# Linear attention times SwiGLU in fp32 on one core: the first part's products and side-work matmuls tied to the written order, the reciprocals in two halves, the masked sum split one place ahead

## The chip, the cores and the metric

The kernel runs on one core of one Trainium2 chip. The metric is device time in microseconds, the median of several runs. Engines are named as in the profile: PE is TensorE (matmuls), PEld its weight loads, DVE is VectorE, ACT is ScalarE, POOL is GpSimd, SP is SyncE, which here issues DMAs only.

## The reference, cut to what matters

```python
xn = _layernorm(x)                                   # x: 2048 x 1024
q, k, v = (xn @ wqkv), in 32 heads of 32
phi = lambda t: jnp.where(t > 0, t + 1, jnp.exp(t)) + 1e-6
pq, pk = phi(q), phi(k)
kv = jnp.einsum("bhsd,bhse->bhde", pk, v);  z = jnp.einsum("bhsd->bhd", pk)
o = jnp.einsum("bhqd,bhde->bhqe", pq, kv) / (jnp.einsum("bhqd,bhd->bhq", pq, z)[..., None] + 1e-6)
s = o @ wo
h = _silu(xn @ w1) * (xn @ w3)                       # w1, w3: 1024 x 3584
return x + s * _silu(h @ w2)
```

All of it is fp32. Most of the arithmetic is in the products of `xn` with `wqkv`, `w1` and `w3` (the first part) and in `h @ w2` and `o @ wo` (the second).

## The kernel before

**Products.** Each fp32 operand is split into a high and a low half (`split`, L83: a copy on ACT makes the high half, a subtraction on DVE the low one), and `mm3` (L94) makes three fp32r matmuls of 128x128 by 128x512 of a pair. `product` (L378) does that for four pieces of the inner dimension: twelve matmuls into one PSUM bank. `gemm` (L399) makes a 2x2 block product from seven such products in Strassen's manner (Winograd's form). It is written in the order B11, T2, T3, T1, B21, T4, B22; the names are those of the weights' combinations, which `Operands.made` (L308) makes a stage ahead. The first product's bank is copied to `u` by ACT, later ones are added to `u` by DVE; B21 goes into the same bank as B11, after the copy; T4 into T3's and B22 into T1's. For two early pairs of keys and values (`early`) B21 comes second.

**The first part** (`half`, L525, twice: 1024 tokens each) runs these products for keys, values, queries and then gate and up (14 pairs of 256 columns). An accumulator's name tells which: `ak0_2` is bank a of the keys of half 0, pair 2; `bk`, `ck`, `dk` are its banks b, c and d (T2 goes into b, T3 and T4 into c, T1 and B22 into d); `v`, `q`, `g`, `u` stand for values, queries, gate and up.

**Side work** goes between the products: `catch_up` (L387) is called once behind nearly every product, and takes one step of a list. One list (`later`) holds, for each pair of keys and values, five steps (`keys_values`): turning a tile of keys and one of values by transposes (`trk`, `trv`, L481), which ACT copies from PSUM into the tile `kvr` (L482, two copies), and one step later the small product `kv` of the two (L514). The `kvr` tile comes from the same pool of eight buffers (`pb`) as the split weights; which buffer a tile gets, the framework decides while it schedules. The other list (`jobs`) is made of generators, which give up their turn at each `yield True`: in half 0 the next half's rows are normalised on DVE (`xn`, L154) and turned (`tA`, L218), then the sums of `w2` are made; in half 1 come the denominators (`den`, L754; their operands `pqs` are split at L91 and L92; the reciprocal at L762 and the store of `r_d`), the merging of `kv` into `wo` (`wp`; the masked sum `kvf`, its split `kvm`, the split of `wo` called `wos`), the division of the queries for the first half of the tokens, and the denominators of the second half.

**What sets the order.** The framework schedules by a simulated timeline: within each engine it puts first what it holds to be ready, unless an edge forbids it. `tc.issue_after(m)` adds such edges: what is traced under it, on m's engine, stands behind m in that engine's order. It is an order, and no wait of its own. Before the change, `catch_up` gave its steps edges to the sums of the products just made (`marks`, on ACT and DVE) and to weight loads (`fetched`, on SP); nothing tied one product to another on PE in the first part. Every engine runs its instructions in the order that was fixed at build time.

**The second part** (L865 on) multiplies `h` by `w2` in four segments and the divided queries by the merged `wo` in a fifth, eight groups of tokens each, with an edge from each product to the one before.

Of the kernel before, what the change touches and what calls it, by code (L numbers as in the profile page):

```python
# [17 lines left out]
C = 512  # L18
H = 32
# [3 lines left out]
def tile_linear_attention_times_swiglu(  # L23
# [10 lines left out]
    nc = tc.nc  # L34
# [250 lines left out]
    fetched, made = [], {}  # L285
# [89 lines left out]
                    else:  # L375
                        yield

    def product(acc, B, A, start, stop=True):  # L378
        K = ND // 2
        for k in range(K):  # L380
            mm3(acc, (B[:, 0, k], B[:, 1, k]), (A[:, 0, k], A[:, 1, k]),
                start=start and k == 0, stop=stop and k == K - 1)

    later = []
    jobs = []

    def catch_up(*marks):  # L387

        if later:
            later.pop(0)()  # L390
        elif jobs:
            job, in_order = jobs[0]
            with ExitStack() as behind:
                for m in marks + (tuple(fetched) if in_order else ()):
                    behind.enter_context(tc.issue_after(m.ins))
                if next(job, None) is None:
                    jobs.pop(0)

    def gemm(B, A, use, early=False, paired=False, own=False):  # L399

        name = B.name
        B.upto("B11")
        u = (st.tile([P, C], F32, tag="own", bufs=1, name=f"u{name}") if own else
             pe.tile([P, C], F32, tag="u", name=f"u{name}"))  # L410
        ba = bank(f"a{name}")
        product(ba, B.upto("B11"), A["A11"], True)
        copied = nc.scalar.copy(out=u, in_=ba)
        if early:
            catch_up(copied)
            yield
            product(ba, B.upto("B21"), A["A12"], False)
            use(0, 0, ba)
            yield
            for _ in B.stages:  # L420
                pass
        else:
            next(stages, None)
            catch_up(copied)
            if paired:
                yield
        bb, bc, bd = (bank(f"{n}{name}") for n in "bcd")
        product(bb, B.upto("T2"), A["S2"], True)
        added = nc.vector.tensor_add(out=u, in0=bb, in1=u)
        next(stages, None)  # L430
        catch_up(copied, added)
        if paired:
            yield
        product(bc, B.upto("T3"), A["S3"], True)
        c22 = small(f"c22{name}")
        added = nc.vector.tensor_add(out=c22, in0=bc, in1=u)
        next(stages, None)
        catch_up(copied, added)
        if paired:
            yield  # L440
        product(bd, B.upto("T1"), A["S1"], True)
        added = nc.vector.tensor_add(out=c22, in0=bd, in1=c22)
        use(1, 1, c22)
        next(stages, None)
        catch_up(copied, added)
        if paired:
            yield
        if not early:
            product(ba, B.upto("B21"), A["A12"], False)
            use(0, 0, ba)  # L450
            next(stages, None)
            catch_up(copied, added)
        if paired:
            yield
        product(bc, B.upto("T4"), A["A22"], False)
        c21 = small(f"c21{name}")
        made[name, "c21"] = added = nc.vector.tensor_add(out=c21, in0=bc, in1=u)
        use(0, 1, c21)
        next(stages, None)
        catch_up(copied, added)  # L460
        if paired:
            yield
        product(bd, B.upto("B22"), A["S4"], False)
        c12 = small(f"c12{name}")
        made[name, "c12"] = added = nc.vector.tensor_add(out=c12, in0=bd, in1=u)
        use(1, 0, c12)
        next(stages, None)
        if name[0] in "gu":
            catch_up(copied, added)
# [264 lines left out]
    def denominators(c):  # L734

        den = []

        def load(j):
            t = job_tile([P, 2, C], f"pqd{j}_{c}")
            nc.sync.dma_start(out=t, in_=pq_d[j // JG][c][:, j % JG:j % JG + 2])  # L740
            return t

        def steps(j, t):
            a = []
            for e in range(2):
                a.append(pb.tile([P, 2, C], FR, tag="b", name=f"pqs{j + e}_{c}"))
                split(a[e], t[:, e], 1e-6)
                yield True
            if not den:
                den.append(bank(f"den{c}"))  # L750
            for e in range(2):
                o = (j + e) * 2 * H
                for i in range(2):
                    nc.tensor.matmul(den[0], lhsT=zb[0][:, o:o + P], rhs=a[e][:, i], skip_group_check=True,  # L754
                                     start=j + e + i == 0, stop=j + e == ND - 1 and i == 1)
            yield True
            if j + 2 == ND:

                r = small(f"r{c}")
                nc.scalar.copy(out=r[:H], in_=den[0][H:2 * H])  # L760
                nc.vector.scalar_tensor_tensor(r[:H], den[0][:H], 1e-6, r[:H], op0=ALU.add, op1=ALU.add)
                nc.vector.reciprocal(r[:H], r[:H])  # L762
                nc.gpsimd.dma_start(out=r_d[c], in_=r[:H])

        return [Job(lambda j=j: load(j), lambda t, j=j: steps(j, t)) for j in range(0, ND, 2)]
# [26 lines left out]
    def merge_wo(k):  # L792

        both = []

        def load(e):
            j = k + e * (ND // 2)
            t = job_tile([P, 2, C], f"wo{j}")
            nc.sync.dma_start(out=t, in_=wo[j * P:(j + 1) * P, :].rearrange("p (n c) -> p n c", c=C))
            return t  # L800

        def steps(e, t):
            both.append(t)
            j = k + e * (ND // 2)
            f = small(f"kvf{j}")[:, :P]
            nc.vector.tensor_mul(f, hmask, kvacc[:, j])
            kvm = st.tile([P, 2, P], FR, tag="kvm", bufs=1, name=f"kvm{j}")
            split(kvm, f)
            o = [pb.tile([P, 2, C], FR, tag="b", name=f"wos{j}_{n}") for n in range(2)]
            for n in range(2):  # L810
                split(o[n], t[:, n])
                yield True
            yield True
            for n in range(2):
                acc = bank(f"wp{j}_{n}")
                mm3(acc, (kvm[:, 0], kvm[:, 1]), (o[n][:, 0], o[n][:, 1]), True, True)
                nc.scalar.copy(out=t[:, n], in_=acc)
                yield True
            if e:
                b = [t[:, n] for t in both for n in range(2)]  # L820
                for n, i in (("B11", 0), ("B21", 2), ("B22", 3)):
                    store(n, b[i])
                yield True
                yield from sums_of(*b)
                yield True
                for n, i in (("T1", 0), ("T3", 1), ("T4", 2), ("T2", 3)):
                    store(n, b[i])
                for _ in range(2):
                    yield True

        def store(n, t):
            nc.gpsimd.dma_start(out=wp_d[n][:, k], in_=t)

        return [Job(lambda e=e: load(e), lambda t, e=e: steps(e, t)) for e in range(2)]


# [81 lines left out]
    def second_weight(i, n, k):  # L918
# [4 lines left out]
                      lambda m, n, i=i: ho_d[i][m // NT][:, m % NT, KEPT.index(n)])  # L923
# [4 lines left out]
    acc = [home.tile([P, 2 if m < NG - 1 else 1, 2, C], F32, tag=f"acc{m}", name=f"acc{m}")  # L928
           for m, home in enumerate(homes)]
# [97 lines left out]
    X, xs = {}, []  # L1027
# [32 lines left out]
    for j, (i, m, n) in enumerate(sequence):  # L1060
        seg = segments[i]
        if n == ORDER[0]:
            parts[m] = attention_tokens(seg, m) if seg is attention else layer_tokens(seg, m, i == 0)
        fetch(j + AHEAD)
        with ExitStack() as order:
            for o in made[i, m, n]:
                order.enter_context(tc.issue_after(o.ins))
            b, start = next(parts[m])
        with ExitStack() as order:
            if j:  # L1070
                order.enter_context(tc.issue_after(multiplied.ins))
            multiplied = seg.product(b, X.pop(j), n, start)
        if m == NG - 1 and i + 1 < len(segments):
            segments[i + 1].place(n)
            segments[i + 1].right(n)
        elif m < NG - 2 and 0 < i < len(layers):
            catch_up(*loads, *made[sequence[j + AHEAD]])
        if j % 2 and (j + 5) // 2 < len(ORDER):
            first_right((j + 5) // 2)
        if n == ORDER[-1]:  # L1080
            next(parts[m])
# [24 lines left out]
```

## Time and profile before

| | us |
|---|---|
| median of 3 runs | 2388.78 (2388.39 to 2388.79) |
| the profiled execution, its own time | 2381.99 |
| its span, first to last instruction | 2380.1 |
| PE busy in the span | 2332.4 |
| DVE busy | 1633.6 |
| ACT busy | 938.0 |

The profiled execution is 6.8 us shorter than the median of the timed runs. The first part ends at about 1670 us of the span. A matmul's record is longer than its turn, since matmuls are pipelined: how fast they follow each other is read from their starts. In rows of the timeline the first number is the start, the second the length, and a bracket at the end gives the idle time of the engine before the row and what ended it. In the views of the profile buffer numbers are left out, so `ak0_2` reads `ak` with the number of its instruction.

### The profile page before, as it was taken

The numbers are of one execution on the slowest core, as the hardware profiler recorded it, in microseconds if no ns is written. First come the engines' busy times: TensorE is split into PE (matmuls) and PEld (weight loads), VectorE is DVE, ScalarE is ACT, GpSimd is POOL, SyncE is SP. The second block draws the span as 40 slices with busy tenths as digits, with TensorE's granted clock in tenths as the row PEclk, the third lists the DMA queues.
The fourth block names the chain that finished last, engine by engine and source line by source line (L and its number), as shares of the span: only waits on it lengthen the run. The fifth ranks groups of instructions, "written<-read, shape, count | busy, mean of one in ns | idle before, by whom it ended". The sixth has DMA issues, their size and how long they took to land.

```text
span 2380.1 us, 29741 instructions
## 1 busy us (share of the span) xinstructions
PE 2332.4 (98%) x10544; PEld 1928.1 (81%) x10544; DVE 1633.6 (69%) x2906; ACT 938.0 (39%) x1595; POOL 289.4 (12%) x359
## 2 busy tenths in 40 slices
PE   7999999999999999999999999999999999999998
PEld 5888888888888888888788888888888887788787
DVE  8755678878888575567877878778436566575644
ACT  5433544443332244445344333344435233243532
POOL 3000111212112110000222212211000000000001
PEclk9999999999999999999999999999999999999999
DMA  3222444547676572433444545544437565554656
GB/s 124 89 97 101 152 151 165 193 155 256 229 240 240 178 271 89 146 118 123 155 165 142 204 157 195 179 143 168 152 98 245 161 192 175 184 189 144 179 155 146
DMA packets 267365, 395.45 MB, mean 166 GB/s; under 512 B 17488, under 2 KB 191824, under 8 KB 266768
## 3 DMA queue, kind: packets, MB, share of 16 engines
q1 hardware_dynamic: 239248, 301.51, 38.9%
q0 software_dynamic: 27968, 92.03, 11.1%
q8 instruction: 83, 1.36, 0.2%
q14 instruction: 66, 0.54, 0.1%
HBM read 271.58 MB, written 140.77 MB: 173 GB/s over the span
## 4 chain that ended last, share of the span: by engine, by line
PE 86%; issue 7%; DMA 3%; DVE 1%; POOL 1%; ACT 1%; SPq 0%; POOLq 0%; DVEq 0%; ACTq 0%
PE cB L99 2%; PE cB L97 2%; PE cB L98 2%; PE dB L99 1%; PE dB L97 1%; PE dB L98 1%; PE kv L514 1%; PE aB L97 1%; PE aB L99 1%; PE aB L98 1%; PE cs L97 1%; PE cs L99 1%; PE cs L98 1%; DMA XA12s<-qs_d 1%; PE den L754 1%
## 5 line engine op out<-in xcount | busy, mean ns | idle before, releaser
L636 POOL DMA_DIRECT2D ho_d<-hs x112 | 101.7, 908 | 84.3 <-DVE hs L609 61.3
L628 POOL DMA_DIRECT2D ho_d<-sg x56 | 51.1, 912 | 446.4 <-DVE sg L623 373.0
L787 POOL DMA_DIRECT2D qs_d<-qd x32 | 27.3, 858 | 534.2 <-DVE qd L611 488.9
L587 POOL DMA_DIRECT2D pq_d<-pq x32 | 17.6, 550 | 483.2 <-DVE pq L475 478.7
L914 DVE TENSOR_TENSOR XA12B<-XA12B 128x512 fp32r<-128x512 f32 (+1 forms) x32 | 19.7, 623 | 53.2 <-ACT XA12B L913 53.2
L626 POOL DMA_DIRECT2D ho_d<-sg x56 | 37.9, 677 | 130.8 <-DVE sg L623 116.3
L97 PE MATMUL aB<-B21B,XA12B 128*128 128x512 f32 x112 | 44.6, 398 | 3.0 <-ACT XA12B L913 2.9
L97 PE MATMUL cB<-T4B,XA22B 128*128 128x512 f32 x112 | 43.8, 391 | 2.4 <-ACT XA22B L913 2.4
L97 PE MATMUL cB<-T2B,XS2B 128*128 128x512 f32 x112 | 44.0, 393 | 1.6 <-ACT cB L967 1.5
L97 PE MATMUL dB<-T1B,XS1B 128*128 128x512 f32 x112 | 44.3, 396 | 1.2 <-ACT XS1B L913 1.2
L99 PE MATMUL dB<-T1B,XS1B 128*128 128x512 f32 x112 | 44.1, 394 | 0.6 <-DVE XS1B L914 0.6
L99 PE MATMUL aB<-B21B,XA12B 128*128 128x512 f32 x112 | 44.4, 397 | 0.0
L98 PE MATMUL aB<-B21B,XA12B 128*128 128x512 f32 x112 | 44.3, 396 | 0.0
L99 PE MATMUL cB<-T4B,XA22B 128*128 128x512 f32 x112 | 43.9, 392 | 0.1
L98 PE MATMUL dB<-T1B,XS1B 128*128 128x512 f32 x112 | 44.0, 393 | 0.0
L99 PE MATMUL cB<-T2B,XS2B 128*128 128x512 f32 x112 | 43.8, 391 | 0.1
L99 PE MATMUL dB<-B22B,XS4B 128*128 128x512 f32 x112 | 43.7, 390 | 0.0
L99 PE MATMUL cB<-T3B,XS3B 128*128 128x512 f32 x112 | 43.7, 390 | 0.0
L98 PE MATMUL cB<-T2B,XS2B 128*128 128x512 f32 x112 | 43.6, 390 | 0.0
L98 PE MATMUL cB<-T4B,XA22B 128*128 128x512 f32 x112 | 43.6, 389 | 0.0
L97 PE MATMUL cB<-T3B,XS3B 128*128 128x512 f32 x112 | 43.6, 389 | 0.0
L98 PE MATMUL dB<-B22B,XS4B 128*128 128x512 f32 x112 | 43.6, 389 | 0.0
(5750 smaller groups left out, 7990.6 us busy)
## 6 DMA issues: line engine op xcount, KB each, us to landing
ho_d<-hs POOLq DMA_DIRECT2D x112, 256.0 KB, 5.8
qs_d<-qd POOLq DMA_DIRECT2D x32, 512.0 KB, 4.1
ho_d<-sg POOLq DMA_DIRECT2D x56, 256.0 KB, 3.5
w<-in_B_w SPq DMA_DIRECT2D x56, 256.0 KB
wt_d<-w SPq DMA_DIRECT2D x28, 512.0 KB
pq_d<-pq POOLq DMA_DIRECT2D x32, 256.0 KB, 2.8
a_dS<-xo SPq DMA_DIRECT2D x16, 512.0 KB
pqd<-pq_d SPq DMA_DIRECT2D x16, 512.0 KB
```

The costliest lines, as they stand in the source:

```text
L97: nc.tensor.matmul(acc, lhsT=wh, rhs=ah, start=start, stop=False, skip_group_check=True)
L98: nc.tensor.matmul(acc, lhsT=wh, rhs=al, start=False, stop=False, skip_group_check=True)
L99: return nc.tensor.matmul(acc, lhsT=wl, rhs=ah, start=False, stop=stop, skip_group_check=True)
L514: nc.tensor.matmul(acc, lhsT=r[:, 1, t], rhs=r[:, 0, t], start=t == 0, stop=t == C // P - 1)
L587: nc.gpsimd.dma_start(out=pq_d[j // JG][2 * h + c][:, j % JG], in_=pq)
L626: nc.gpsimd.dma_start(out=ho_d[i][2 * h + c][:, :, 0, k], in_=halves[:, :, 0])
L628: nc.gpsimd.dma_start(out=ho_d[i][2 * h + c][:, :, 1:3, k], in_=halves)
L636: nc.gpsimd.dma_start(out=ho_d[i][2 * h + c][:, :, 3 + 2 * e:5 + 2 * e, k], in_=o[e].rearrange("p (g n s) -> p g n s", n=2, s=P))
L754: nc.tensor.matmul(den[0], lhsT=zb[0][:, o:o + P], rhs=a[e][:, i], skip_group_check=True, start=j + e + i == 0, stop=j + e == ND - 1 and i ...
L787: nc.gpsimd.dma_start(out=qs_d[m][:, :, k], in_=t.rearrange("p a (n s) -> p (a n) s", s=P))
L914: return high, nc.vector.tensor_sub(out=lo, in0=src, in1=hi.bitcast(F32))
```

## The change

- `product` ties its matmuls behind the last matmul of the product made before (`multiplied`), except in the early gemms (`free`); a product that is made so becomes the next one's mark.
- `catch_up` ties what its step issues on PE behind the last product made, too: transposes, `kv`, `den` and `wp` can't stand ahead of it. They can still stand later than written.
- The reciprocal of 32x512 is made in two halves of 32x256, and each has a turn of its own ahead of it: two more `yield True` at the end of each of the four chunks of denominators.
- In `merge_wo` a turn is given up between the split of the masked sum and that of `wo`: eight more turns.
- In the second part the mark becomes a list; its edges are the same.

```diff
+    multiplied = []
+
+    def product(acc, B, A, start, stop=True, free=False):
         K = ND // 2
-        for k in range(K):
-            mm3(acc, (B[:, 0, k], B[:, 1, k]), (A[:, 0, k], A[:, 1, k]),
-                start=start and k == 0, stop=stop and k == K - 1)
+        with ExitStack() as order:
+            for m in () if free else multiplied:
+                order.enter_context(tc.issue_after(m.ins))
+            for k in range(K):
+                last = mm3(acc, (B[:, 0, k], B[:, 1, k]), (A[:, 0, k], A[:, 1, k]),
+                           start=start and k == 0, stop=stop and k == K - 1)
+        multiplied[:] = [last]
...
         if later:
-            later.pop(0)()
+            with ExitStack() as behind:
+                for m in multiplied:
+                    behind.enter_context(tc.issue_after(m.ins))
+                later.pop(0)()
         elif jobs:
...
-                for m in marks + (tuple(fetched) if in_order else ()):
+                for m in marks + tuple(multiplied) + (tuple(fetched) if in_order else ()):
...
-        product(ba, B.upto("B11"), A["A11"], True)
+        product(ba, B.upto("B11"), A["A11"], True, free=early)
...
-                nc.vector.reciprocal(r[:H], r[:H])
+                for o in range(0, C, C // 2):
+                    yield True
+                    nc.vector.reciprocal(r[:H, o:o + C // 2], r[:H, o:o + C // 2])
                 nc.gpsimd.dma_start(out=r_d[c], in_=r[:H])
...
             split(kvm, f)
+            yield True
             o = [pb.tile([P, 2, C], FR, tag="b", name=f"wos{j}_{n}") for n in range(2)]
```

The other six calls of `product` in `gemm` get `free=early` as well. The change lengthens the file: L97 to L99 keep their numbers, the transposes of L481 are at L490 after it, the copies of L482 at L491, `kv` of L514 at L523, `den` of L754 at L763.

What stands on PE before, in the keys of pair 2 (half 0), from the transposes of one step to the second `kv`; of each product only the first matmul is shown:

```order
L481 MATMUL trk0_2_0_1196<-ident_63,pk0_2_0_537 128x128 x4
L481 MATMUL trv0_2_0_1202<-ident_63,v0_1_590 128x128 x4
L97 MATMUL bk0_2__1208<-S2_0_177,T2k0_2__1076 128x512
...
L97 MATMUL ak0_2__1177<-A12_0_180,B21k0_2__1097 128x512
...
L514 MATMUL kv0_2_0_1229<-kvr0_2_0_1195 128x128 x4
L481 MATMUL trk0_3_1_1236<-ident_63,pk0_3_1_981 128x128 x4
L481 MATMUL trv0_3_1_1242<-ident_63,c22v0_1__1118 128x128 x4
L97 MATMUL ck0_2__1209<-S3_0_178,T3k0_2__1078 128x512
...
L514 MATMUL kv0_3_1_1265<-kvr0_3_1_1235 128x128 x4
```

And the same place after the change:

```order
L490 MATMUL trk0_2_0_1196<-ident_63,pk0_2_0_537 128x128 x4
L490 MATMUL trv0_2_0_1202<-ident_63,v0_1_590 128x128 x4
L97 MATMUL bk0_2__1208<-S2_0_177,T2k0_2__1076 128x512
...
L523 MATMUL kv0_2_0_1229<-kvr0_2_0_1195 128x128 x4
L490 MATMUL trk0_3_1_1236<-ident_63,pk0_3_1_981 128x128 x4
L490 MATMUL trv0_3_1_1242<-ident_63,c22v0_1__1118 128x128 x4
L97 MATMUL ck0_2__1209<-S3_0_178,T3k0_2__1078 128x512
...
L523 MATMUL kv0_3_1_1265<-kvr0_3_1_1235 128x128 x4
```

The product B21, which stood between T2 and `kv0_2_0`, is gone from there; it now stands behind T1, as it is written. The second `kv` has T3 alone ahead of it, before and after.

Two rows of PE's order in the gate of pair 2 (half 0), with the transposes of the next half's rows (`tA111_1`) and the products around them, before:

```order
L97 MATMUL ag0_2__3228<-A11_0_176,B11g0_2__3051 128x512
...
L97 MATMUL ag0_2__3228<-A12_0_180,B21g0_2__3113 128x512
...
L218 MATMUL tA111_1_3246<-ident_63,xn1_0_3054 128x128 x4
L97 MATMUL bg0_2__3255<-S2_0_177,T2g0_2__3094 128x512
L98 MATMUL bg0_2__3255<-S2_0_177,T2g0_2__3094 128x512
```

And after:

```order
L99 MATMUL ag0_2__3228<-A11_0_176,B11g0_2__3051 128x512
L218 MATMUL tA111_1_3246<-ident_63,xn1_0_3054 128x128 x4
L97 MATMUL bg0_2__3255<-S2_0_177,T2g0_2__3094 128x512
L98 MATMUL bg0_2__3255<-S2_0_177,T2g0_2__3094 128x512
L99 MATMUL bg0_2__3255<-S2_0_177,T2g0_2__3094 128x512
```

B21 no longer stands between B11 and the transposes.

ACT's order behind the copy of the first denominators (`r0`), before:

```order
L760 COPY r0_9100<-den0_8834 32x512
L91 ACTIVATE pqs0_1_9107<-pqd0_1_9029 128x512
L89 CAST B22g1_0__9129<-wg1_0__8810 128x512
L413 COPY ug1_0__9159<-ag1_0__9160 128x512
L473 ACTIVATE pq1_6_1_9124<-c21q1_3__9122 128x512
```

And after:

```order
L769 COPY r0_9100<-den0_8834 32x512
L89 CAST B22g1_0__9122<-wg1_0__8810 128x512
L89 CAST B11u1_0__9147<-wu1_0__8980 128x512
L422 COPY ug1_0__9150<-ag1_0__9151 128x512
L482 ACTIVATE pq1_6_1_9117<-c21q1_3__9115 128x512
L482 ACTIVATE pq1_7_0_9140<-c12q1_3__9138 128x512
L483 ACTIVATE pq1_6_1_9117<-pq1_6_1_9117 128x512
L483 ACTIVATE pq1_7_0_9140<-pq1_7_0_9140 128x512
L89 CAST T1u1_0__9166<-wu1_0__8980 128x512
L91 ACTIVATE pqs0_1_9173<-pqd0_1_9029 128x512
```

The split of `pqs0_1`, the first operand of the second chunk's denominators, moved from the place behind `r0` to one behind the split of T1 of the up weights.

More of the change, by code (lines that the diff above doesn't have):

```diff
@@ L376, in in_turn @@
                         yield
-    def product(acc, B, A, start, stop=True):
+    multiplied = []
+    def product(acc, B, A, start, stop=True, free=False):
         K = ND // 2
-        for k in range(K):
-            mm3(acc, (B[:, 0, k], B[:, 1, k]), (A[:, 0, k], A[:, 1, k]),
-                start=start and k == 0, stop=stop and k == K - 1)
+        with ExitStack() as order:
[5 more added lines that the diff above has]
+        multiplied[:] = [last]
     later = []
@@ L416, in gemm @@
             yield
-            product(ba, B.upto("B21"), A["A12"], False)
+            product(ba, B.upto("B21"), A["A12"], False, free=early)
             use(0, 0, ba)
@@ L427, in gemm @@
         bb, bc, bd = (bank(f"{n}{name}") for n in "bcd")
-        product(bb, B.upto("T2"), A["S2"], True)
+        product(bb, B.upto("T2"), A["S2"], True, free=early)
         added = nc.vector.tensor_add(out=u, in0=bb, in1=u)
@@ L433, in gemm @@
             yield
-        product(bc, B.upto("T3"), A["S3"], True)
+        product(bc, B.upto("T3"), A["S3"], True, free=early)
         c22 = small(f"c22{name}")
@@ L440, in gemm @@
             yield
-        product(bd, B.upto("T1"), A["S1"], True)
+        product(bd, B.upto("T1"), A["S1"], True, free=early)
         added = nc.vector.tensor_add(out=c22, in0=bd, in1=c22)
@@ L448, in gemm @@
         if not early:
-            product(ba, B.upto("B21"), A["A12"], False)
+            product(ba, B.upto("B21"), A["A12"], False, free=early)
             use(0, 0, ba)
@@ L454, in gemm @@
             yield
-        product(bc, B.upto("T4"), A["A22"], False)
+        product(bc, B.upto("T4"), A["A22"], False, free=early)
         c21 = small(f"c21{name}")
@@ L462, in gemm @@
             yield
-        product(bd, B.upto("B22"), A["S4"], False)
+        product(bd, B.upto("B22"), A["S4"], False, free=early)
         c12 = small(f"c12{name}")
@@ L1069, in tile_linear_attention_times_swiglu @@
         with ExitStack() as order:
-            if j:
-                order.enter_context(tc.issue_after(multiplied.ins))
-            multiplied = seg.product(b, X.pop(j), n, start)
+            for o in multiplied if j else ():
+                order.enter_context(tc.issue_after(o.ins))
+            multiplied[:] = [seg.product(b, X.pop(j), n, start)]
         if m == NG - 1 and i + 1 < len(segments):
```

## The prediction

> **What bounds the kernel now.** First the page's head and its slices, for the engine that is full. The first line gives span and instructions, the next busy time and share of each engine, the last the granted clock in 40 slices.
>
> ```profile
> span 2380.1 us, 29741 instructions
> PE 2332.4 (98%) x10544; PEld 1928.1 (81%) x10544; DVE 1633.6 (69%) x2906; ACT 938.0 (39%) x1595; POOL 289.4 (12%) x359
> ...
> PEclk9999999999999999999999999999999999999999
> ```
>
> TensorE is busy 98% of the span at full clock. Less than 50 us can be won at all, and whatever makes TensorE wait longer is lost in full. So I read next the waits of TensorE (total, times, longest), and keep those inside the first part.
>
> ```profile
> PE wp L97 <- ACT kvm L89: 1.8, 1, 1.8
> PE kv L514 <- ACT kvr L482: 1.7, 1, 1.7
> ...
> PE den L754 <- ACT pqs L91: 1.0, 1, 1.0
> ...
> PE wp L97 <- ACT wos L89: 1.0, 3, 0.5
> ...
> PE ag__4220 L97 <- ACT ug__4219 L413: 0.7, 1, 0.7
> PE ag__3228 L97 <- ACT ug__3227 L413: 0.7, 1, 0.7
> PE ak__7068 L97 <- ACT uv__7085 L413: 0.6, 1, 0.6
> ```
>
> These sum to 7.5 us: all that a better order of the first part can remove, beside the start-up. The question is rather what the old order hides. For that I read the timeline around a kv product (start, length, instruction, idle time before it), and with it two rows from a place where TensorE had waited.
>
> ```profile
> 129.28 0.39 PE L99 MATMUL bk__1208<-S,T2k__1076 128*128 128x512 f32 x1
> 129.51 0.39 PE L97 MATMUL ak__1177<-A,B21k__1097 128*128 128x512 f32 x1
> ...
> 132.23 1.05 PE L514 MATMUL kv<-kvr 128*128 128x128 f32 x8
> ...
> 380.61 0.50 PE L97 MATMUL ag__3228<-A,B21g__3113 128*128 128x512 f32 x1 [0.68 <-ACT ug__3227 L413]
> 380.95 0.39 PE L98 MATMUL ag__3228<-A,B21g__3113 128*128 128x512 f32 x1
> ```
>
> ```profile
> 129.77 0.60 ACT L482 ACTIVATE kvr<-trk 128x512 f32<-128x512 f32 x1 [1.17 <-PE bk__1208 L99]
> 130.26 0.59 ACT L482 ACTIVATE kvr<-trv 128x512 f32<-128x512 f32 x1
> ```
>
> Twelve matmuls take 132.23 - 129.51 = 2.72 us, 0.227 each. A record's 0.39 outlasts its turn by 0.16, so a wait costs its idle time plus 0.16; and the first matmul behind a wait takes 380.95 - 380.61 = 0.34, which is 0.11 beyond its turn (the restart, below). The two ACT copies into kvr begin only when bk's last matmul has ended (129.67), though their transposes ran before bk: kvr's buffer is the one bk's T2 operand left. The B21 product, brought forward, covers them.
>
> **The ties, part by part.** *kv without its cover.* In the changed order kv stands right behind the T2 product at seven places (kv0_2_0, kv0_5_0, kv0_7_1, kv1_1_1, kv1_3_1, kv1_5_1, kv1_7_1). The view of line 482 names them: the same copies wait for exactly those seven T2 products.
>
> ```profile
>   PE trk L481: 12.8, 17
>   PE bk__7733 L99: 2.6, 1
>   PE bk__8093 L99: 2.6, 1
>   PE bq__8453 L99: 2.6, 1
>   PE bk__7373 L99: 1.8, 1
> ...
>   PE bv__1776 L99: 1.4, 1
>   PE bq__2077 L99: 1.3, 1
>   PE bk__1208 L99: 1.2, 1
> ```
>
> Three more rows: the T2-kv place at 887 us, the second kvr of a pair, and the one kv that waits already.
>
> ```profile
> 887.22 0.39 PE L97 MATMUL ak__7342<-A,B21k__7255 128*128 128x512 f32 x1
> ...
> 887.92 0.59 ACT L482 ACTIVATE kvr<-trv 128x512 f32<-128x512 f32 x1
> ...
> 133.82 0.60 ACT L482 ACTIVATE kvr<-trk 128x512 f32<-128x512 f32 x1 [0.77 <-PE trk L481]
> ...
> 192.00 0.82 PE L514 MATMUL kv<-kvr 128*128 128x128 f32 x5 [1.74 <-ACT kvr L482]
> ```
>
> The price: kv would be due at 129.51 and the copies end at 130.85; with some 0.04 to start and 0.11 for the restart that is 1.49. At 887 us it is 888.51 + 0.04 - 887.22 + 0.11 = 1.44. I take 1.47 each: 7 x 1.47 = 10.3 us.
>
> The second kvr of a pair took over the first one's buffer before, and was copied as soon as its transposes had run (133.82). In the changed build it has the buffer of T3, and T3 is read by the product just ahead of its kv (kv0_3_1, kv0_6_0, kv1_0_0, kv1_2_0, kv1_4_0, kv1_6_0). So the same wait comes six times more: 8.8 us. Together 13 x 1.47 = 19.1 us. Bounds: 1.3 each (no restart), or 2.0 as at 192.00 (1.74 + 0.16 + 0.11). I keep 1.47, since the copies that wait are the same ones, in the same place behind T2. That kv at 192.00 keeps its neighbours, and so its wait.
>
> *The transposes of xn.* At 380 and at 499 us the old order put B21 behind B11, and paid for it with a wait for the copy of u. The tie moves B21 back; the next on TensorE are then the transposes tA of xn.
>
> ```profile
> 379.54 0.39 PE L99 MATMUL ag__3228<-A,B11g__3051 128*128 128x512 f32 x1
> 498.72 0.39 PE L99 MATMUL ag__4220<-A,B11g__4043 128*128 128x512 f32 x1
> ```
>
> ```profile
> 381.50 1.75 DVE L154 TENSOR_SCALAR xn<-xn,mom 128x1024 f32<-128x1024 f32 x2
> ...
> 500.68 1.75 DVE L154 TENSOR_SCALAR xn<-xn,mom 128x1024 f32<-128x1024 f32 x2
> ```
>
> VectorE's order up to xn is the same in both builds. tA is due at 379.54 + 0.23 = 379.77; the first of the two normalisations ends at 381.50 + 0.87 = 382.37. That is 2.64 with the start, 2.75 with the restart, against 0.68 + 0.16 + 0.11 = 0.95 before: +1.8. At 499 us likewise (501.55 against 498.95): together +3.6. Bounds: -1.9 for the two, should VectorE get there sooner, to +5.3, should tA wait for both normalisations (0.87 more each).
>
> *B21 at 848 us* goes back too; nothing is late there instead, since VectorE's T2 split stands ahead of three small sums that it stood behind (hs, 0.4 each): -0.9 (0.64 + 0.16 + 0.11).
>
> *den and the reciprocals.* The first den1 matmul moves from ahead of T2 to behind T3.
>
> ```profile
> 1105.97 0.39 PE L99 MATMUL ag__9160<-A,B11g__8982 128*128 128x512 f32 x1
> ...
> 1108.59 3.33 DVE L762 RECIPROCAL r<-r 32x512 f32<-32x512 f32 x1
> ...
> 1112.39 0.67 DVE L429 TENSOR_TENSOR ug__9159<-bg__9183,ug__9159 128x512 f32<-128x512 f32 x1
> ...
> 1106.65 0.62 ACT L91 ACTIVATE pqs<-pqd 128x512 fp32r<-128x512 f32 x1
> ```
>
> Its pqs split, on ACT at 1106.65 now, then stands behind the split of T1u, whose source VectorE makes after both halves of the reciprocal (adjacent there, 3.3 us as before) and the add to ug: 1111.9 + 0.6 + 0.7 = 1113.2, two ACT splits to 1114.3. den1 is due at 1105.97 + 0.23 + 24 x 0.227 = 1111.65. Late by 2.7, 2.8 with the restart, against 0.97 + 0.16 + 0.11 = 1.24 before: +1.6 (bounds -1.2, no wait at all, to +3, if each half takes 0.7 longer than half of 3.33). The halves of r1 to r3 hold up what stands behind them on VectorE, 1.7 us at a time; in the written order a sum has two products, 5.4 us, until its bank is used again. That hides them; without it each would cost up to 1.7. r_d's store moves later on POOL with the stores queued behind it, and what it holds is read only much later, by the divisions.
>
> *The masked sum one place ahead* takes away the 1.8 on kvm (2.07 lost) and the longest wait on wos (0.75); the second halves of wp stand close behind their splits at four places instead of two, 0.52 each as now for 0.24 idle. 3.9 before, 2.1 after: -1.8 (0 to -3.9). The 16 extra places move den3's end by 13 products; four products are left behind it, so no side work runs over, and SP and POOL have the same order in the second part.
>
> Sum: 19.1 + 3.6 - 0.9 + 1.6 - 1.8 = +21.6 us on the profiled execution's 2381.99 (its span is 2380.1). The median of the runs, 2388.78, lies 6.8 above that; with it 2410.4, call it 2410.
>
> **The clock.** How long TensorE may stand still is the term that I know least. Mean granted clock is the third figure from the right:
>
> ```profile
> 2043.70:2047.00 3.30, 0.38 (x2) 0.00 (x0) 0.01 (x1) 0.55 (x2) 0.00 (x0) 0.86 0.90 340
> 2047.00:2053.00 6.00, 5.99 (x14) 4.74 (x15) 4.52 (x9) 1.93 (x4) 0.00 (x0) 0.51 0.52 153
> 2221.50:2224.20 2.70, 0.29 (x2) 0.00 (x0) 2.70 (x4) 2.27 (x5) 0.00 (x0) 1.00 0.65 240
> ```
>
> A stop of 2.9 us halved the clock for six (14 matmuls, 3.2 us' worth: 2.8 us lost); one of 2.4 (2.70 less the end of the matmul before it) did not. My three long new stops, idle 2.5 to 2.6, lie between: nearer to the harmless one, so I add nothing. [...]
>
> **The rivals.** (a) *Only the seven.* If the second copies of a pair still start after their transposes, as at 133.82, six stops go: 2410.4 - 8.8 = 2401.6. For it: 17 of the copies wait so today. Against: the build's buffers.
> (b) *The clock drops* at the three long stops: 3 x 2.8 more, 2419. Against it the row at 2221.
> (c) *Faster.* ACT and VectorE, freed from matmuls that came early, run far enough ahead for kv and xn: the copies start at the transposes, 2.7 us ahead of kv, and xn over 2.6 us sooner. It decides where copies end before the product does. Then only the removals count: -1.9 - 0.9 - 1.24 - 1.8 = -5.8, 2383. Against it the 1.17 us for which ACT stood idle waiting for bk: being early doesn't help it.
> (d) *It does nothing:* the order hardly changes a time, 2389. The moved rows speak against.
>
> **How the numbers follow.** Forecast 0.64; (a) 0.15; (b) 0.12; (c) 0.05; (d) 0.04. Bounds of the forecast's own terms: 17 to 26 for kv, -1.9 to 5, -1.2 to 3, -3.9 to 0. They don't fall on one side together; 2403 to 2418 for the forecast. To take in (a) and (b): 2400 to 2420. About 0.2%, 4.8 us, is what a measurement can tell from no change: faster 0.05, same 0.05, slower 0.90.
>
> **What would show it.** Right: the waits view has "PE kv <- ACT kvr" some 14 times, 17 us or so idle, where it had one; tA waits for xn twice, 2.5 us each; no product waits for a copy of u; kvm is gone from the list. Wrong: kv waits once, or the copies at line 491 wait for transposes alone; or the clock row shows halves in the first part.

## The result, and the profile after

The changed kernel takes 2415.6 us, the median of four runs (2413.3 to 2417.3), against 2388.8 before: a ratio of 1.0118 (95% interval 1.0105 to 1.0130), 26.8 us slower. Forecast were 2410 us and 21.6 us of loss, so the sign and the main causes were right and the size was 5 short. The profiled execution of before lies 6.8 us below its kernel's median, that of after 0.5 below; so two profiles differ by more than the medians do.

First the head of the page after: the span is 32.9 us longer, and TensorE, with the same 10544 matmuls, is busy for 97% of it.

```profile
span 2413.0 us, 29770 instructions
PE 2342.6 (97%) x10544; PEld 1931.9 (80%) x10544; DVE 1641.6 (68%) x2910; ACT 938.0 (39%) x1595; POOL 289.0 (12%) x359
```

Then TensorE's waits after (us in total, times, longest), those that are new or changed:

```profile
PE kv L523 <- ACT kvr L491: 17.3, 14, 1.7
...
PE tA L218 <- DVE xn L154: 5.0, 2, 2.5
...
PE den L763 <- ACT pqs L91: 2.6, 1, 2.6
PE bk__7103 L99 <- DVE T2k__6952 L90: 2.4, 1, 2.4
...
PE wp L97 <- ACT wos L89: 1.2, 4, 0.3
```

Where kv had one wait of 1.7 it now has fourteen with 17.3. The transposes of xn wait twice, 2.5 each; no product waits for a copy of u; kvm has left the list. The row of `bk__7103`, the T2 product of the first keys of half 1, was not foreseen. The timeline around the first of the new kv stops shows the cause that the prediction gave:

```profile
132.99 0.39 PE L99 MATMUL bk__1208<-S,T2k__1076 128*128 128x512 f32 x1
...
133.47 0.60 ACT L491 ACTIVATE kvr<-trk 128x512 f32<-128x512 f32 x1 [2.56 <-PE bk__1208 L99]
133.97 0.59 ACT L491 ACTIVATE kvr<-trv 128x512 f32<-128x512 f32 x1
134.61 1.16 PE L523 MATMUL kv<-kvr 128*128 128x128 f32 x8 [1.24 <-ACT kvr L491]
```

ACT stands idle for 2.56 us until bk's last matmul has ended, then fills the buffer that bk's operand left (the first experiment tests this), and kv, now right behind bk, waits for it.

For a full account I took for every matmul the time since the start of the one before, less the median for its shapes (0.227 for 128x512), and summed the excess by what released it (profiled executions, us):

| excess of TensorE | before | after | difference | forecast |
|---|---|---|---|---|
| kv waits for kvr | 1.9 | 19.4 | +17.5 | +19.1 with restarts |
| restarts and other small gaps, first part | 5.8 | 7.8 | +2.0 | (above) |
| at the two xn places | 1.7 | 5.3 | +3.6 | +3.6 |
| first keys and values of half 1 | 0.8 | 2.6 | +1.8 | -0.9 |
| den | 1.1 | 2.7 | +1.6 | +1.6 |
| wp | 3.4 | 1.9 | -1.6 | -1.8 |
| half clock, first part | 0 | 4.2 | +4.2 | 0 |
| the first 100 us | 17.0 | 20.3 | +3.3 | 0 |
| second part | 22.4 | 22.4 | 0 | 0 |
| rest | 0.5 | 0.4 | -0.1 | |
| sum | 54.7 | 87.0 | +32.3 | +21.6 |

Four terms stand within 0.4 us. Two were missed: the stop at T2 of half 1, and the clock. The 3.3 us of the start stand behind a weight load, that of `wv__699`: VectorE waits 2.05 us for it before and 2.84 after, and TensorE, at `bv__803` behind it, 1.5 and 3.1; after the longer wait a window at half clock follows, at 71.99 us, 1.6 lost. Two kernels below without any tie (the masked sum alone, the halves alone) wait 2.6 and 2.7 there and have 19.5 and 19.8 in the first 100 us, so it needs no tie.

### The profile page after: what moved, and what is told of

Its sections match the earlier page's. It is cut to its first block, busy times and chain, and to the rows that moved or that the text cites. A ratio compares the mean times of both kernels' runs of the same rounds, so it can differ in the third digit from the quotient of the medians.

```text
span 2413.0 us, 29770 instructions
## 1 busy us (share of the span) xinstructions
PE 2342.6 (97%) x10544; PEld 1931.9 (80%) x10544; DVE 1641.6 (68%) x2910; ACT 938.0 (39%) x1595; POOL 289.0 (12%) x359
## 4 chain that ended last, share of the span: by engine, by line
PE 43%; issue 8%; DMA 3%; DVE 1%; ACT 1%; SPq 0%; POOL 0%; POOLq 0%; DVEq 0%; ACTq 0%
PE cB L99 2%; PE cB L97 2%; PE cB L98 2%; PE dB L99 1%; PE dB L97 1%; PE dB L98 1%; PE aB L97 1%; PE aB L98 1%; PE aB L99 1%; DMA XA12s<-qs_d 1%; PE cs L97 1%; PE cs L98 1%; PE cs L99 1%; PE ds L99 1%; PE ds L98 1%
## 5 line engine op out<-in xcount | busy, mean ns | idle before, releaser
L523 PEld LDWEIGHTS kv<-kvr 128*128 128x128 f32 x256 | 32.4, 191 | 24.4 <-ACT kvr L491 23.0
L523 PE MATMUL kv<-kvr 128*128 128x128 f32 x256 | 35.1, 280 | 17.3 <-ACT kvr L491 17.3
L97 PE MATMUL aB<-B21B,XA12B 128*128 128x512 f32 x112 | 44.4, 396 | 4.2 <-ACT XA12B L925 4.2
L97 PE MATMUL cB<-T2B,XS2B 128*128 128x512 f32 x112 | 44.1, 394 | 1.2 <-ACT cB L979 1.1
L97 PE MATMUL cB<-T4B,XA22B 128*128 128x512 f32 x112 | 43.7, 390 | 1.4 <-ACT XA22B L925 1.4
L99 PE MATMUL cB<-T3B,XS3B 128*128 128x512 f32 x112 | 43.8, 391 | 1.2 <-DVE XS3B L926 1.2
L97 PE MATMUL dB<-T1B,XS1B 128*128 128x512 f32 x112 | 43.8, 391 | 0.7 <-ACT XS1B L925 0.7
L99 PE MATMUL aB<-B21B,XA12B 128*128 128x512 f32 x112 | 44.2, 394 | 0.0
L99 PE MATMUL dB<-T1B,XS1B 128*128 128x512 f32 x112 | 43.9, 392 | 0.2 <-DVE XS1B L926 0.2
L97 PE MATMUL cB<-T3B,XS3B 128*128 128x512 f32 x112 | 43.7, 390 | 0.3 <-ACT XS3B L925 0.3
L99 PE MATMUL cB<-T4B,XA22B 128*128 128x512 f32 x112 | 43.8, 391 | 0.0
L99 PE MATMUL dB<-B22B,XS4B 128*128 128x512 f32 x112 | 43.7, 390 | 0.0
L99 PE MATMUL cB<-T2B,XS2B 128*128 128x512 f32 x112 | 43.6, 389 | 0.0
```

The source lines that it names most:

```text
L97: nc.tensor.matmul(acc, lhsT=wh, rhs=ah, start=start, stop=False, skip_group_check=True)
L99: return nc.tensor.matmul(acc, lhsT=wl, rhs=ah, start=False, stop=stop, skip_group_check=True)
L523: nc.tensor.matmul(acc, lhsT=r[:, 1, t], rhs=r[:, 0, t], start=t == 0, stop=t == C // P - 1)
```

## The clock, seen on a grid

Granted clock in windows of 3.413 us (first figure the window's length, then PE's busy time; the clock is third from the right), in pairs: one with a new stop, and the one behind it. After:

```profile
389.43:392.85 3.42, 1.71 (x8) 1.09 (x6) 3.42 (x10) 0.59 (x1) 1.94 (x3) 1.00 1.01 343
392.85:396.26 3.41, 2.63 (x14) 2.26 (x15) 3.41 (x7) 1.21 (x2) 1.12 (x2) 1.00 0.56 227
512.31:515.73 3.42, 1.25 (x8) 1.12 (x9) 3.42 (x7) 1.50 (x3) 2.16 (x3) 1.00 0.91 348
515.73:519.14 3.41, 3.41 (x10) 2.67 (x9) 3.33 (x7) 0.03 (x1) 0.91 (x1) 0.50 0.10 40
863.89:867.30 3.41, 0.98 (x5) 0.64 (x4) 3.41 (x8) 0.93 (x2) 1.12 (x2) 1.00 1.05 410
867.30:870.71 3.41, 3.41 (x10) 2.64 (x9) 2.41 (x6) 0.01 (x1) 1.67 (x2) 0.50 1.06 413
1143.78:1147.19 3.41, 1.14 (x5) 0.97 (x6) 3.41 (x7) 1.15 (x2) 1.62 (x3) 1.00 0.28 98
1147.19:1150.60 3.41, 3.41 (x10) 2.66 (x9) 1.78 (x3) 0.00 (x0) 0.00 (x0) 0.50 0.26 102
```

The stops at 391 and at 512 us are the same transposes waiting for the same xn, 2.48 us idle each. The first left the clock at full speed, the second halved it for exactly one window: eight matmuls start in it, 0.427 us apart, where fifteen fit, 1.6 us lost (the x10 of its row takes in two that began before it). The first is divided by the edge at 392.85, the second lies in one window. All half-clock stretches of this execution, seven of 3.413 us each and the one in which it ends, begin on one grid of 3.413 us, to within 0.006: from the first record of the clock, at 20.79 us, to the last of these, at 2410.12, it is 700 windows. So what decides in these runs is how much of one window TensorE stands idle, counting each matmul as busy for its turn. In the thirteen profiles of this study, from 22 us of the span on and without the stretch in which each execution ends, 67 half-clock stretches each follow a window with about 2.04 us or more of idle time, and none of the 66 windows at full clock with 1.5 to about 2.04 us idle is followed by one. The limit that these profiles show is 2.04 us, 60% of the window, give or take 0.03 by how a matmul's turn is counted.

## The experiments

**The buffer of kvr.** The tile is taken from the side jobs' three buffers, which are idle while keys and values are made; the order of kv behind the thirteen products stays.

```diff
-            rows[n, c] = pb.tile([P, 2, C // P, P], F32, tag="b", name=f"kvr{name}")
+            rows[n, c] = job_tile([P, 2, C // P, P], f"kvr{name}")
```

> The changed kernel with one edit: the tile kvr comes from the buffers of the side jobs (tag job, three buffers, idle while keys and values are made) and no longer from the pool that holds the split weights. Order of the products as in the changed kernel; each kv of the thirteen stays right behind the same T2 or T3 product. Theory (the copies into kvr wait for the product whose operand held the buffer): the copies start at their transposes, the thirteen stops go, 13 x 1.45 = 18.9 us, so 2415.6 - 18.9 = 2396.7 (2394 to 2400), and the waits view has PE kv <- ACT kvr at most twice. Rival 1 (ACT itself is late there, whatever the buffer): the stops stay, 2413 to 2418. Rival 2 (the seven behind T2 are a matter of the buffer, the six behind T3 of something else): 2405.

Measured: 2388.6 us, ratio to before 1.0004 (0.9992 to 1.0015). No kv waits for kvr any more, and what line 491 waits for is its transposes alone, where in the changed kernel its view begins with products (us in total, times; changed kernel first):

```profile
  PE ck__1209 L99: 3.0, 1
```

```profile
  PE trk L490: 17.8, 18
```

So all thirteen stops, the six behind T3 as well, came from the buffer; both rivals fall. The gain is 27.0 where 18.9 was expected, and the time lies outside the range of the theory. The account of its profile against that of after: 19.4 at kv, 1.8 of restarts and small gaps, 2.0 at T2 of half 1, where the weight load was issued 5.5 us behind the one before it and not 7.3, and 3.4 in the first 100 us, which differ in the same way between kernels without ties; other parts give back 0.9. The rest of the gap between 27.0 and 18.9 the runs do not split further.

**Which of the ties.** Twice a part of the change alone: product behind product, and side work behind products. Both without the halves and the earlier masked sum.

```diff
-                for m in marks + tuple(multiplied) + (tuple(fetched) if in_order else ()):
+                for m in marks + (tuple(fetched) if in_order else ()):
```

(and no tie around `later.pop(0)()`: products alone)

```diff
-            for m in () if free else multiplied:
+            for m in ():
```

(side work alone)

> The changed kernel with the ties of product to product alone: catch_up ties no side work behind a product, the reciprocal is whole, the masked sum is split where it was. Theory (the loss hangs on the order of the products, the B21 product going back behind T1): the thirteen stops at kv, two at xn and the one at T2 of the first keys of half 1 stay; the wait for kvm returns (+1.9) and the long one at den goes back to 1.2 (-3.0): 2414.5 (2411 to 2418). Rival (side work tied behind products is what lost the time): 2388 to 2400.

> The changed kernel with the ties of side work behind products alone: products are not tied to each other, the reciprocal is whole, the masked sum is split where it was. Theory (as for the product ties): B21 stays ahead of kv and the time is that of the kernel before, 2389 (2387 to 2391). Rival (the side work's ties cost by themselves): 2395 or more.

Measured: products alone 2424.6 us, ratio 1.0141 (1.0123 to 1.0160); side work alone 2388.5, ratio 0.9993 (0.9984 to 1.0003). The waits view of products alone:

```profile
PE kv L520 <- ACT kvr L488: 17.2, 14, 1.7
...
PE tA L218 <- DVE xn L154: 4.9, 2, 2.5
...
PE dg__10872 L97 <- DVE c22g__10903 L448: 2.4, 1, 2.4
PE bk__7103 L99 <- DVE T2k__6952 L90: 2.3, 1, 2.3
...
PE wp L97 <- ACT kvm L89: 1.8, 1, 1.8
```

The loss hangs on the tie of product to product, which sends B21 back behind T1; the side work's ties move nothing that matters. Products alone lost 10 more than expected, outside the range of the theory. Some 4 of that are the stop at `dg`, 2.4 idle, and the half clock behind it, 1.6, which no theory had named; on VectorE its sum stands behind a division that waits for a load:

```profile
1365.97 0.69 DVE L790 SCALAR_TENSOR_TENSOR qd<-qd 128x512 f32<-128x512 f32 x1 [7.27 <-DMA qd<-pq_d]
1366.58 0.68 DVE L448 TENSOR_TENSOR c22g__10903<-dg__10872,c22g__10903 128x512 f32<-128x512 f32 x1
...
1367.32 0.50 PE L97 MATMUL dg__10872<-S,B22g__10810 128*128 128x512 f32 x1 [2.40 <-DVE c22g__10903 L448]
```

The profiled execution, 8.6 us above its kernel's median, also has 12 us more of waits and half clock in the second part; the runs show no cause for these.

**The weight load on SP.** In the unforeseen stop, SP's rows of before and of after (timeline; S is loaded in fours):

```profile
820.66 0.67 SPq L301 DMA_DIRECT2D wk__6614<-in_A_wqkv  x1
821.96 2.85 SPq L301 DMA_DIRECT2D wv__6875<-in_A_wqkv  x1
824.90 10.15 SPq L565 DMA_DIRECT2D S<-a_dS  x8
```

```profile
835.17 0.38 SPq L301 DMA_DIRECT2D wk__6614<-in_A_wqkv  x1
836.51 5.87 SPq L574 DMA_DIRECT2D S<-a_dS  x4
842.48 0.76 SPq L301 DMA_DIRECT2D wv__6875<-in_A_wqkv  x1
...
854.79 0.62 ACT L89 CAST B11v__6897<-wv__6875 128x512 fp32r<-128x512 f32 x1 [3.32 <-DMA wv__6875<-in_A_wqkv]
...
865.82 0.69 DVE L90 TENSOR_TENSOR T2k__6952<-wk__6614,T2k__6952 128x512 fp32r<-128x512 f32 x1
...
866.56 0.50 PE L99 MATMUL bk__7103<-S,T2k__6952 128*128 128x512 f32 x1 [2.43 <-DVE T2k__6952 L90]
```

The change moved the load of the first values' weights behind four loads of S3 on SP's queue: 7.3 us from wk to wv in place of 1.3. ACT waits 3.3 us for them, the splits behind on ACT and VectorE slide, and T2's low half comes when TensorE has stood for 2.4 us. The experiment ties the loads from S3 on behind that weight load:

```diff
...
+            for i, n in enumerate(AOPS):
+                with ExitStack() as behind:
+                    if i > 1:
+                        behind.enter_context(tc.issue_after(loaded["v1_0_"].ins))
...
```

> The changed kernel with one edge more: on SP the loads of S3 and of the operands behind it, for the second 1024 tokens, stand behind the weight load of the first values of that half, as in the kernel before; in the changed kernel four of them stand ahead of it. Theory (the stop of 2.43 us idle at T2 of the first keys of half 1 comes from that weight load landing late): the stop goes, 2.6 to 2.8, and with it a stretch at half clock, up to 1.7, if one followed: 2415.6 - 4.2 = 2411.4 (2410 to 2414). Rival (VectorE or the full DMA queues make T2 late, wherever the load stands): the stop stays, 2414 to 2418.

Measured: 2412.7 us, ratio 1.0103 (1.0088 to 1.0118). The wait shrinks to

```profile
PE bk__7103 L99 <- DVE T2k__6952 L90: 0.7, 1, 0.7
```

and no stretch at half clock follows it. The medians differ by 2.9 and the intervals overlap, so the stop is settled by the profile, its price only roughly by the times: 1.7 of idle time, and 1.6 of clock where the stop fell into one window.

**Three places later.**

```diff
+            if i % 2:
+                yield True
             a11, a12, a21, a22 = (t[c][:, n * C:(n + 1) * C] for c in range(2) for n in range(2))
...
+            if (j, c) == (0, 1):
+                yield True
             if not den:
```

> The changed kernel with three places more: the transposes of xn come one product later at the two tiles that were waited for, and the first den matmul of the second chunk one product later. Theory (they stand one product, 2.72 us, too early, and are 2.6 to 2.7 late): three stops go, 2 x 2.63 + 2.73 = 8.0, and the stretches at half clock behind them, 1.6 each, of which each timed run has two or three: 2415.6 - 8.0 - 4.0 = 2403.6 (2401 to 2408). Rival 1 (what is late moves with them): 2413 to 2417. Rival 2 (stops of this length never change the clock; the half clock came from something else): 2407.6.

Measured: 2402.8 us, ratio 1.0064 (1.0050 to 1.0078), 12.8 less than the changed kernel. The wait for den is gone, and of the two for xn one is left:

```profile
PE kv L525 <- ACT kvr L493: 17.3, 14, 1.7
PE bk__7103 L99 <- DVE T2k__6952 L90: 2.5, 1, 2.5
...
PE tA L218 <- DVE xn L154: 1.0, 1, 1.0
```

In idle time that is 6.6 us. With 0.16 for each of the two stops that are gone and their restarts it is near 7, which leaves some 6 for the clock and for chance; without the clock 2407.6 was due. The profiles show the clock's share: the half-clock windows behind these two stops, at 515.73 and 1147.19 us after, have no counterpart here, and the only one left in the first part behind the start, at 860.08, follows the stop at T2. That is 3.2 of the 6. Both rivals fall.

**All three cures.** Buffers apart, weight load first, three places later, with all the ties kept.

> The changed kernel with the buffers of kvr apart, the weight load ahead of S3 on SP, and the three places later, all at once. Theory (the stops are the whole loss and add up): from the 2388.6 of the kernel with kvr apart 8.0 of stops, 0.6 at T2, 0.3 of restarts and two or three stretches at half clock of 1.6 go: 2375.5 (2372 to 2380), faster than the kernel before by 0.5%. Rival (the waits come back elsewhere once these are gone): 2382 to 2389.

Measured: 2378.7 us (2377.1 to 2381.4), ratio 0.9961 (0.9947 to 0.9974): faster than before. Of waits in the first part behind the start these are left, with no stretch at half clock among them:

```profile
PE wp L97 <- ACT wos L89: 1.4, 5, 0.3
...
PE tA L218 <- DVE xn L154: 1.0, 1, 1.0
```

Once each stop is covered, the tied order is not slow; the ties cost only what they uncovered. Whether they also bring something, the last experiments show: the two small parts and the buffers apart, without ties, measure the same.

**The copies twice.** To lengthen the thirteen stops, and to see what the clock does with stops of one length:

```diff
-        nc.scalar.activation(dst, p_.rearrange("p (t d) -> p t d", t=C // P), AF.Identity, bias=bias)
+        for _ in range(2):
+            nc.scalar.activation(dst, p_.rearrange("p (t d) -> p t d", t=C // P), AF.Identity, bias=bias)
```

> The changed kernel in which each of the two ACT copies into kvr is made twice, with the same result. Theory of the stops: the thirteen stops at kv grow by 1.04 to 1.2 us each, +13.5 to +15.6. Theory of the clock (a window of 3.41 us on a fixed grid in which TensorE stands idle for more than 2.05 us is followed by one at half clock): of thirteen stops of 2.3 to 2.4 us idle about half, six or seven, fall that way, +1.6 each, +10.5: together 2415.6 + 25 = 2441 (2435 to 2446), and the profile's half-clock stretches start on the grid. Rival (the clock falls only after a stop of 2.9 us or more): no stretch behind a kv, 2429 to 2432.

Measured: 2453.2 us, ratio 1.0271 (1.0257 to 1.0285), 12 above the forecast and outside its range. The thirteen stops grew to 2.15 to 2.21 idle, 0.98 each, 12.7 together. But the fourteenth grew from 1.74 to 3.23, and seven new ones came, all behind B22, six of them of 1.6 us, where the copies had ended in time before: TensorE's excess at kv rose from 19.4 to 45.1. The clock went as the grid says, and it parts the theories. The timeline, and the windows on this execution's grid around its two stops:

```profile
207.03 1.16 PE L524 MATMUL kv<-kvr 128*128 128x128 f32 x8 [3.23 <-ACT kvr L492]
218.74 1.99 PE L524 MATMUL kv<-kvr 128*128 128x128 f32 x8 [2.15 <-ACT kvr L492]
```

```profile
201.79:205.21 3.42, 2.01 (x18) 1.73 (x16) 1.17 (x3) 1.81 (x4) 0.00 (x0) 1.00 0.02 5
205.21:208.62 3.41, 1.59 (x14) 1.59 (x15) 1.65 (x5) 1.77 (x4) 0.00 (x0) 1.00 0.49 141
208.62:212.03 3.41, 3.40 (x18) 2.57 (x16) 0.86 (x3) 3.29 (x7) 0.00 (x0) 1.00 1.16 455
215.45:218.86 3.41, 1.25 (x7) 0.72 (x6) 1.86 (x5) 2.06 (x4) 0.00 (x0) 1.00 0.00 0
218.86:222.27 3.41, 3.41 (x13) 3.02 (x14) 0.98 (x2) 0.62 (x1) 0.00 (x0) 0.50 0.00 0
```

A stop of 3.23 us, divided by an edge into 1.58 and 1.94 of its windows' idle time, changed nothing; one of 2.15 inside a window halved the clock. Five of the thirteen did, against six or seven expected. The length of a stop alone does not decide.

**The two small parts without ties.** Both, each alone, and both with the buffers of kvr apart:

```diff
-                nc.vector.reciprocal(r[:H], r[:H])
+                for o in range(0, C, C // 2):
+                    yield True
+                    nc.vector.reciprocal(r[:H, o:o + C // 2], r[:H, o:o + C // 2])
...
             split(kvm, f)
+            yield True
```

> The kernel before with the two small parts of the change alone: reciprocals in two halves with places of their own, and the masked sum split a place ahead; no ties. Theory (each part has its own cost, and the ties made the loss): kvm leaves the waits view, 2.0 us, four short waits on wos stay, so 2388.8 - 1.9 = 2386.9 (2385 to 2389). Rival (the places moved by twenty-four steps make new waits of VectorE's or of the loads): slower than before, 2390 to 2393.

> The kernel before with the masked sum split one place ahead and nothing else. The two small parts together measured 7.1 less than before, against 1.9 expected. Theory (the sum of the stops in the profile: kvm goes, 1.96, and the longer wait on wos): 2387.7 - 2.1 = 2385.6 (2384 to 2387). Rival 1 (the masked sum brings all of the seven): 2380.7. Rival 2 (it brings nothing, the gain is the reciprocals'): 2387.7.

> The kernel before with the reciprocals in two halves, each at a place of its own, and nothing else. Theory (the sum of the stops: the wait at den1, 1.13, goes): 2387.7 - 1.1 = 2386.6 (2385 to 2388). Rival 1 (the halves, with their eight more places and what these move in the second chunk of work, bring most of the seven): 2380.7 to 2383. Rival 2 (each half holds up what stands behind it on VectorE): 2388 or more.

> The kernel before with the two small parts of the change and with the buffers of kvr apart; no ties. Theory (each stop counts by itself): from the 2380.7 of the two small parts alone the one wait for kvr, 1.9, goes: 2378.8 (2377 to 2381). Rival (with kvr out of the pool the scheduler moves other work, and the waits come back): 2381 to 2386.

| kernel | median us | ratio to before (95%) |
|---|---|---|
| both parts | 2380.7 | 0.9963 (0.9949 to 0.9977) |
| masked sum alone | 2386.1 | 0.9995 (0.9985 to 1.0005) |
| halves alone | 2387.1 | 0.9996 (0.9985 to 1.0007) |
| both, kvr apart | 2378.2 | 0.9965 (0.9954 to 0.9977) |

Both parts together came out 4 below the theory's range, the others inside theirs. Each alone moves the places of the rest so that another stop comes. The waits of the masked sum alone, and of the halves alone:

```profile
PE den L754 <- ACT pqs L91: 2.0, 2, 1.0
```

```profile
PE cg__13075 L97 <- DVE c22g__13110 L436: 2.3, 1, 2.3
```

With the masked sum alone den waits twice where it waited once. With the halves alone the two halves of a later reciprocal stand next to each other again on VectorE, ahead of a sum that a product needs:

```profile
1592.83 3.34 DVE L764 RECIPROCAL r<-r 32x256 f32<-32x256 f32 x2
...
1596.71 0.67 DVE L436 TENSOR_TENSOR c22g__13110<-cg__13075,ug__13048 128x512 f32<-128x512 f32 x1
...
1597.44 0.80 PE L97 MATMUL cg__13075<-A,T4g__12981 128*128 128x512 f32 x1 [2.29 <-DVE c22g__13110 L436]
```

Together neither stop is there. The first part's waits and half clock are 8.9 us before, 7.5 with the masked sum alone, 9.5 with the halves alone and 5.7 with both. That explains 3.2 of the 7.1 us that the medians show for both; where the rest comes from the runs do not show, and the median of before itself has runs from 2383.9 to 2392.8 behind it. kvr apart takes away the last kv wait, but 2378.2 against 2380.7 lies inside the intervals. The tied kernel with all three cures and this untied one are equal within the measurement, both 0.35 to 0.4% faster than before. So this gain is the small parts', and no run shows one of the ties.

## Why the prediction was right, and where it fell short

- *kv without its cover*: right in cause, count and price. Thirteen new stops with 1.17 or 1.24 idle, 1.43 to 1.49 each with 0.16 and 0.10 of restart, against 1.47. That the six behind T3 wait like the seven behind T2, read from the buffers of the changed build, held; rival (a) is out.
- *Transposes of xn*: right, 2.48 idle twice, +3.6.
- *den*: right, 2.56 idle, +1.6, with the copy for pqs behind that for T1u on ACT as described. *Masked sum*: -1.6 against -1.8; four short waits of 0.3.
- *B21 at 848 us*, "nothing is late there instead": this step failed, by 2.7 us and a stretch at half clock. It looked at VectorE's order alone. What was late came from SP: a weight load had moved behind four loads of S3. For the side jobs the prediction did follow SP's and POOL's queues; for this edge it did not.
- *The clock*: "nearer to the harmless one, so I add nothing" failed. The two rows that it rested on, 2.9 idle and 2.4 idle, differ in how they lie on the grid: 2.16 idle in one window at 2043, and 1.95 at 2221. Two of the three stops it named halved the clock, and the unforeseen one did. A stop of 2.64 us counted in turns (2.48 idle and 0.16) is harmless only where an edge leaves less than the measured 2.04 on both sides, which is 1.44 us of the 3.41 that an edge can fall on: by this estimate it costs 1.6 us in 58% of cases, 0.9 on average, and four such stops 3.7. With that and the 2.7 the sum is 21.6 + 6.4 = 28.0, against 26.8 measured. That it comes so near is in part luck: the account of the two profiles has 32.3 to explain, 29.0 without the start. The prediction's own sign of being wrong, half clock in the first part, did come, and for this step it was a true one. Rival (b) had the mechanism, at 2.8 for each stop in place of 1.6.
- *Rival (c), faster*: neither the copies nor xn came early enough; kv and the transposes waited as priced. *The second part*: as forecast, no difference in the profiles.

## What to carry to other kernels

An edge that puts products into the written order takes away the work that the scheduler had slid between a producer and its consumer: before adding it, list each consumer that lands right behind the product that frees its producer's buffer. Then cover the stops by a buffer, a place or an earlier load: here that turned a loss of 1.2% into the gain of 0.4% that the small parts have without ties, too. Follow a changed order through the queue of loads, too.

## What was not expected of the hardware

- In the thirteen profiles the clock fell behind windows of a fixed 3.413 us grid that had about 2.04 us or more of idle time, and not by the length of one stop: with the copies twice 3.23 us passed and 2.15 did not. The grid lies differently in the span of before and of after (edges at 18.57 and at 20.79 us), and of two stops of 2.48 us idle after, the one at 391 us left the clock at full speed and the one at 512 us lost 1.6 us by it.
- The way back to full speed asked for more than the way down. Of most half-clock stretches one window is all; ten of the 67 last two (before, 2046 to 2053). In the thirteen profiles a window at half clock with 0.88 us or more of idle time was followed by another one in all ten cases, and one with 0.75 us or less by full clock in all others; here a matmul of 128x512 counts as busy for 0.427 us.
- Each of the thirteen executions begins at half clock, which the clock column doesn't show: the clock's records begin only at 18 to 21 us of the span (18.57 before, 20.79 after), and the column takes the time ahead of them as full (1.00 from 11 to 14 us, before). The starts tell it: before, the transposes of 128x128 follow each other at 0.213 us until 18.57 us and at 0.109 from there on; after, at 0.213 up to the last of them at 20.15. In all thirteen profiles the last window ahead of that moment has less than 0.5 us of idle time, and the one ahead of it 1.06 or more.
